# Where the reciprocals of the softmax denominators are taken: on columns before a transpose, or on rows after it

## The chip, the cores and the metric

The kernel runs on one core of a Trainium2 chip. Each core has a matrix engine (TensorE, "PE" in the profile, with its weight loads "PEld"), a vector engine (VectorE, "DVE"), an activation engine (ScalarE, "ACT"), a general engine (GpSimd, "POOL") and a queue that here issues all DMAs (SyncE, "SP"). Each engine works through its own instructions in the order in which they were written; an instruction that has to wait holds up all that stand behind it on its engine. The metric is the device time of one execution in microseconds.

## The reference

A clustered attention is followed by two gated feed-forward layers. The change lies in the attention, of which this is the end (2 batches, 8 heads, 768 tokens, head size 64):

```python
scores = np.where(mask, scores, -1000000000.0)
scores = scores - np.max(scores, axis=-1, keepdims=True)
attn = np.exp(scores)
attn = attn / (np.sum(attn, axis=-1, keepdims=True) + 1e-09)
return np.matmul(attn, v).astype(np.float32)
```

The two layers behind it (1536 tokens of width 512; 2048 and 1536 hidden features) take most of the time and are not touched.

## The kernel before, in words

The attention takes its heads in 8 pairs. A pair is worked in two halves of 384 query rows, so there are 16 halves, and a half in 6 steps: 3 blocks of 128 query rows for each of the two heads. That gives 96 steps, numbered n = 0 to 95 here; two of them make one turn of the loop at L558.

Step n puts on the engines, in this order:
- `scores` (L341): PE forms 128 x 768 scores in PSUM, in one of two buffers `s_ps`; L347 and L351 are its matmuls.
- `maximum` (L356): DVE takes the row maxima from PSUM (L359).
- `transposes` (L395) of step n - 2: PE transposes the exponentials `p` in two groups (L405); ACT copies them out (L410), or DVE copies one group (L408) in some steps.
- `exponentials` (L363): ACT forms exp(s - max), which needs the maximum; its accumulator leaves the row's sum as one column of the tile `st` (L367). The buffer `s_ps` is free after this, so PE's scores of step n + 2 wait for it.

When the 6 steps of a half are through, `st[:, 1, :]` holds 128 x 6 denominators. In step n = 6, 12, ..., 96, `reciprocals` (L372) adds 1e-9 on DVE (L374) and takes the reciprocals of the 128 x 6 tile (L377). One step later (n = 7, 13, ..., 97), `spread` (L379) transposes them on PE to 6 x 128 (L382), copies them on ACT out of PSUM to `rs` (L384), and SP writes them to DRAM (L386). `bring_back` (L389) reads them back, each row over 64 partitions, into `rb`. `normalised` (L422) multiplies a half's output in PSUM by `rb` on DVE (L424), and `split_x` on POOL cuts the result in two parts (L438, L439). A half's output is ready, and L424 stands, at the end of a turn whose second step is n = 13, 19, ..., that is directly behind the `spread` of the following half.

Beside these, `background` (L500) hands out other work by step: loads and splits of the next pair's q and k on POOL (L247 to L266), the cluster masks of the next pair on DVE (L287 to L332), and the first 9 weight blocks of the feed-forward layer (steps in `early`, L496). Such a block is loaded into the only buffer `raw` (L65), shifted by ACT (L69), worked by DVE (L78, L82), and split by POOL (L88, L93). The next block's load waits until L82 is through. The steps n0 of the blocks are 20, 32, 44, 56, 68, 84, 87, 90 and 93: ACT's part stands in step n0, DVE's in n0 + 1 and n0 + 2, after the step's `spread`.

The order of all this is written out by hand; no scheduler changes it.

Of the kernel before, what the change touches and what calls it, by code (L numbers as in the profile page):

```python
# [8 lines left out]
F32 = mybir.dt.float32  # L9
F32R = mybir.dt.float32r  # L10
AF = mybir.ActivationFunctionType
ALU = mybir.AluOpType
# [8 lines left out]
def tile_kernel(ctx, tc, q_t, k_t, q_s, k_s, v_l, cent, w_in, w_out, a_co, b_co, w_gate, w_val, w_o2, out):  # L21
    nc = tc.nc
# [3 lines left out]
    P = 128  # L26
# [12 lines left out]
    def r32(ap):  # L39
        return ap.bitcast(F32)  # L40
# [84 lines left out]
    def pool(stack, name, bufs, side, space=None):  # L125
        kw = {} if space is None else {"space": space}
        return stack.enter_context(tc.tile_pool(name=name, bufs=bufs, side=side, reuse_waits="tile", **kw))

    stage_pools(A, "left", 1, 1)
    base = pool(A, "base", 1, "left")  # L130
# [16 lines left out]
    live = {}  # L147
    pairs = [(b, hp) for b in range(B) for hp in range(H // 2)]
    order = [(b, hp, half, i, e) for b, hp in pairs for half in range(2) for i in range(HB) for e in range(2)]
    PER = 2 * HB  # L150
# [36 lines left out]
    ident = base.tile([P, P], F32, name="ident")  # L187
    make_identity(nc, ident)

    def t_tile(name):  # L190
        return ps_t.tile([P, HB, P], F32, tag="t", name=name)

    def keep_warm(n, to):
        for _ in range(n):
            for j in range(HB):
                nc.tensor.transpose(to[:, j, :], ident, ident)
# [14 lines left out]
    for e in range(2):  # L211
# [2 lines left out]


    sq = base.tile([P, D], F32, name="sq")
    ss = base.tile([P, 4], F32, name="ss")
    nc.vector.memset(ss[:, 3:4], 1e-36)
    nc.scalar.activation(out=sq, in_=cn, func=AF.Square, accum_out=ss[:, 0:1])
    nc.scalar.activation(out=ss[:, 1:2], in_=ss[:, 0:1], func=AF.Ln, bias=ss[:, 3:4])  # L220
# [3 lines left out]
        out=ss[:, 2:3], in0=ss[:, 0:1], scalar=ss[:, 2:3], in1=ss[:, 1:2], op0=ALU.mult, op1=ALU.add  # L224
# [7 lines left out]
    for e in range(2):  # L232
        nc.vector.tensor_copy(
            out=ct[e * D:(e + 1) * D, :, e, :], in_=ct_ps.rearrange("p (h e c) -> p h e c", e=2, c=NC)[:, :, e, :]
# [106 lines left out]
    def scores(b, hp, half, i, e):  # L341
        t = heads[b, 2 * hp + e]
        s_ps = ps_s.tile([P, S], F32, tag="s", name="s_ps")
        q0 = half * HALF + i * P
        qs = slice(q0, q0 + P)
        for lo, hi in CUT:
            nc.tensor.matmul(s_ps[:, lo:hi], t["q1"][:, qs], t["k1"][:, lo:hi], start=True, stop=False)  # L347
        if (b, hp, half, i, e) == order[0]:
            keep_warm(1, fill)
        for lo, hi in CUT:  # L350
            nc.tensor.matmul(s_ps[:, lo:hi], t["q2"][0:KM, qs], t["k2"][0:KM, lo:hi], start=False, stop=True)  # L351
        if (i, e) == (0, 0):
            live["st", b, hp, half] = st_p.tile([P, 3, PER], F32, tag="st", name="st")
        live["s", b, hp, half, i, e] = s_ps

    def maximum(b, hp, half, i, e):  # L356
        st = live["st", b, hp, half]
        k = e * HB + i
        nc.vector.tensor_reduce(  # L359
            out=st[:, 0, k:k + 1], in_=live["s", b, hp, half, i, e], axis=AX.X, op=ALU.max, negate=True  # L360
        )

    def exponentials(b, hp, half, i, e):  # L363
        st = live["st", b, hp, half]
        k = e * HB + i
        p = live["p", b, hp, half, i, e] = p_p.tile([P, S], F32, tag="p", name="p")
        nc.scalar.activation(  # L367
            out=p, in_=live.pop(("s", b, hp, half, i, e)), func=AF.Exp, bias=st[:, 0, k:k + 1],
            accum_out=st[:, 1, k:k + 1],
        )  # L370

    def reciprocals(b, hp, half):  # L372
        st = live["st", b, hp, half]
        nc.vector.tensor_scalar(  # L374
            out=st[:, 1, :], in0=st[:, 1, :], scalar1=1.0, scalar2=1e-9, op0=ALU.mult, op1=ALU.add
        )
        nc.vector.reciprocal(out=st[:, 2, :], in_=st[:, 1, :])  # L377

    def spread(b, hp, half):  # L379
        st = live.pop(("st", b, hp, half))  # L380
        r_ps = t_tile("r_ps")[0:PER, 0, :]
        nc.tensor.transpose(r_ps, st[:, 2, :], ident)  # L382
        rs = rs_p.tile([PER, P], F32, tag="rs", name="rs")
        nc.scalar.copy(out=rs, in_=r_ps)  # L384
        rd = tc.dram_tile([2, HALF], F32, name="rd")
        nc.sync.dma_start(out=rd.rearrange("e (i p) -> (e i) p", p=P), in_=rs)  # L386
        live["rd", b, hp, half] = rd

    def bring_back(b, hp, half):  # L389
        rd = live.pop(("rd", b, hp, half))  # L390
        rb = live["rb", b, hp, half] = rb_p.tile([P, HALF], F32, tag="rb", name="rb")
        for e in range(2):
            nc.sync.dma_start(out=rb[e * D:(e + 1) * D, :], in_=rd[e:e + 1, :].to_broadcast([D, HALF]))

    def transposes(b, hp, half, i, e, on_dve):  # L395
        p = live.pop(("p", b, hp, half, i, e))
        if i == 0:
            live["pt", b, hp, half, e] = pt_p.tile([P, NB, HALF], F32, tag="pt", name="pt")
        pt = live["pt", b, hp, half, e]
        qc = slice(i * P, (i + 1) * P)  # L400
        for g in range(2):
            t_ps = t_tile("t_ps")
            for j in range(HB):
                kb = g * HB + j
                nc.tensor.transpose(t_ps[:, j, :], p[:, kb * P:(kb + 1) * P], ident)  # L405
            ks = slice(g * HB, (g + 1) * HB)
            if g == 1 and on_dve:
                nc.vector.tensor_copy(out=pt[:, ks, qc], in_=t_ps)  # L408
            else:
                nc.scalar.copy(out=pt[:, ks, qc], in_=t_ps)  # L410
# [11 lines left out]
    def normalised(b, hp, half):  # L422
        x = live["x", b, hp, half] = x_p.tile([P, HALF], F32, tag="x", name="x")
        nc.vector.tensor_tensor(  # L424
            out=x, in0=live.pop(("o", b, hp, half)), in1=live.pop(("rb", b, hp, half)), op=ALU.mult
        )

    def split_x(b, hp, half):
        x = live.pop(("x", b, hp, half))
        done = 0  # L430
        while done < HALF:
            t, o = divmod(b * S + half * HALF + done, T)
            n = min(HALF - done, T - o)
            if t not in x_hl:
                x_hl[t] = xy.tile([P, 2, NCC, T], F32R, tag="xy", name="xhl")
            hi = x_hl[t][:, 0, hp, o:o + n]
            src = x[:, done:done + n]
            nc.gpsimd.tensor_scalar(out=hi, in0=src, scalar1=1.0, scalar2=0.0, op0=ALU.mult, op1=ALU.add)  # L438
            nc.gpsimd.tensor_tensor(out=x_hl[t][:, 1, hp, o:o + n], in0=src, in1=r32(hi), op=ALU.subtract)  # L439
            done += n  # L440
# [7 lines left out]
    for e, t in enumerate((h0, h1)):  # L448
# [6 lines left out]
            out=t["k2"][0:D, :], in0=xk1[0:D, :] if e else xk, in1=r32(t["k1"][0:D, :]), op=ALU.subtract  # L455
# [7 lines left out]
        out=h0["q1"][up, :], in0=xs[0][0:D, :], scalar=scale, in1=r32(h0["q1"][0:D, :]),  # L463
        op0=ALU.mult, op1=ALU.subtract,
# [85 lines left out]
    def next_weighted():  # L550
        if pv:
            step = pv.pop(0)
            weighted(*step)
            if step[3] == NB - 1:
                return step[:3]


    for n0 in range(0, len(order) + LAG, 2):  # L558
        for n in (n0, n0 + 1):
            if n < len(order):  # L560
                scores(*order[n])
                maximum(*order[n])
            if n == 1:
                keep_warm(3, fill)
            if n >= LAG:
                transposes(*order[n - LAG], n % (2 * PER) in dve_evac)
            if n < len(order):
                exponentials(*order[n])
            if n % PER == 0 and n:
                reciprocals(*order[n - 1][:3])  # L570
            if n % PER == 1 and n > 1:
                spread(*order[n - 2][:3])
            if n % PER == BB and n > PER:
                bring_back(*order[n - BB - 1][:3])
            for engine in ("dma", "pe", "dve", "pool", "act"):
                background(n, engine)
        finished = next_weighted()
        finished = next_weighted() or finished
        if finished:
            normalised(*finished)  # L580
            split_x(*finished)
        if n >= LAG and (n - LAG) % PER == PER - 1:
            pv.extend([order[n - LAG][:3] + (kb,) for kb in range(NB)])
# [275 lines left out]
```

## Time and profile before

| what | value |
|---|---|
| median of 3 runs | 815.94 us (814.78 to 818.19) |
| the profiled execution | 815.9 us |
| its span, first to last instruction | 814.1 us |
| granted TensorE clock | 1.0 of full speed over the span |
| PE busy | 790.4 us (97%) |
| DVE busy | 592.6 us (73%) |
| ACT busy | 454.0 us (56%) |
| POOL busy | 329.9 us (41%) |

The attention fills about the first 240 us of the span. PE is nearly always busy, so the time is set by PE and by those places where PE stands still for another engine. A row of the timeline gives the start, the duration, the engine, the line, the operation with its tiles, and in brackets the idle time of that engine just before and what ended it.

### The profile page before, as it was taken

The page shows a single profiled execution, that of the slowest core. Times are in us where ns is not written, and L with a number is a line of the kernel's source. Part 1 is how long each engine was busy: PE and PEld are TensorE (multiplying, and loading weights), DVE is VectorE, ACT ScalarE, POOL GpSimd, SP SyncE. Part 2 cuts the span into 40 slices and gives each one's busy share as a digit, 9 for nine tenths or more (in the row PEclk, how much of TensorE's full clock was granted, in tenths as well). Part 3 has the DMA queues.
Part 4 walks back from the last instruction along what each step waited for, and adds up shares of the span by engine and source line. Part 5 has one row for each costly group of instructions (what it writes and reads, how often), then busy time and mean ns, then how long its engine had stood idle before and what let it go on. Part 6 is the DMA issues. An engine that isn't in the chain of part 4 may idle for free.

```text
span 814.1 us, 10999 instructions
## 1 busy us (share of the span) xinstructions
PE 790.4 (97%) x3912; PEld 614.3 (75%) x3912; DVE 592.6 (73%) x888; ACT 454.0 (56%) x862; POOL 329.9 (41%) x286
## 2 busy tenths in 40 slices
PE   5999999999999899999999999999999999999998
PEld 4766666666667788878878787888888888888886
DVE  6888788778559999999999989775545564533435
ACT  5777766777767788777776768544222232221111
POOL 3666585678232333545453343322223332321112
PEclk9999999999999999999999999999999999999999
DMA  5366335533223221220312001311121211100004
GB/s 162 112 204 198 118 113 191 175 107 121 74 96 125 78 75 57 76 75 30 104 52 77 2 27 52 104 53 65 67 77 52 77 53 52 52 27 1 1 2 154
DMA packets 26551, 67.91 MB, mean 83 GB/s; under 512 B 4448, under 2 KB 9536, under 8 KB 26496
## 3 DMA queue, kind: packets, MB, share of 16 engines
q1 hardware_dynamic: 26496, 67.21, 25.0%
q8 instruction: 31, 0.51, 0.3%
q14 instruction: 24, 0.20, 0.1%
HBM read 59.48 MB, written 3.19 MB: 77 GB/s over the span
## 4 chain that ended last, share of the span: by engine, by line
PE 70%; DVE 22%; ACT 3%; issue 3%; POOL 2%; DMA 1%; DVEq 0%; POOLq 0%; ACTq 0%
PE h_ps L617 30%; PE acc L693 19%; PE o_ps L416 7%; PE t_ps L405 5%; PE s_ps L347 4%; PE s_ps L351 3%; DVE td L653 3%; DVE td L656 2%; DVE g L650 2%; DVE tq L636 2%; DVE st L359 2%; DVE tp L639 2%; DVE c L78 2%; DVE h_ps L640 2%; ACT p L367 1%
## 5 line engine op out<-in xcount | busy, mean ns | idle before, releaser
L617 PE MATMUL h_ps<-yhl,w 128*128 128x512 f32 x864 | 202.0, 389 | 0.0
L617 PEld LDWEIGHTS h_ps<-yhl,w 128*128 128x128 f32 x864 | 162.0, 188 | 34.1 <-DVE yhl L725 0.3
L693 PE MATMUL acc<-g,w 128*128 128x512 f32 x576 | 141.7, 392 | 7.3 <-POOL g L661 7.0
L617 PE MATMUL h_ps<-xhl,w 128*128 128x512 f32 x576 | 138.6, 390 | 0.0
L93 POOL TENSOR_TENSOR w<-c,w 128x512 fp32r<-128x512 f32 x68 | 94.1, 1384 | 103.1 <-ACT w L90 102.4
L693 PEld LDWEIGHTS acc<-g,w 128*128 128x128 f32 x576 | 107.1, 188 | 34.2 <-POOL g L661 11.5
L617 PEld LDWEIGHTS h_ps<-xhl,w 128*128 128x128 f32 x576 | 107.9, 188 | 24.1 <-issue 1.8
L359 DVE TENSOR_REDUCE st<-s_ps 128x1 f32<-128x768 f32 x96 | 91.2, 951 | 31.3 <-PE s_ps L351 30.8
L661 POOL TENSOR_TENSOR g<-td,tr 128x512 fp32r<-128x512 f32 x46 | 59.6, 1296 | 130.9 <-DVE td L656 119.9
L693 PE MATMUL acc<-w,g 128*128 128x512 f32 x432 | 103.3, 389 | 0.0
L709 POOL TENSOR_TENSOR part<-ts,part 128x512 f32<-128x512 f32 x34 | 46.0, 1372 | 134.0 <-ACT ts L708 133.8
L708 ACT COPY ts<-acc 128x512 f32<-128x512 f32 x34 | 20.0, 590 | 142.6 <-PE acc L693 142.6
L367 ACT ACTIVATE p<-s_ps,st 128x768 f32<-128x768 f32 x96 | 87.5, 912 | 20.3 <-DVE st L359 19.3
L693 PEld LDWEIGHTS acc<-w,g 128*128 128x128 f32 x432 | 81.1, 188 | 16.8
L410 ACT COPY pt<-t_ps 128x384 f32<-128x384 f32 x160 | 70.1, 484 | 33.9 <-PE t_ps L405 33.6
L711 DVE TENSOR_TENSOR part<-acc,part 128x512 f32<-128x512 f32 x38 | 26.0, 686 | 82.5 <-PE acc L693 82.4
L405 PE MATMUL t_ps<-ident,p 128*128 128x128 f32 x576 | 79.1, 273 | 0.9 <-ACT pt L410 0.8
L416 PE MATMUL o_ps<-pt,v 128*64 128x384 f32 x384 | 72.3, 498 | 0.0
L405 PEld LDWEIGHTS t_ps<-ident,p 128*128 128x128 f32 x576 | 66.8, 141 | 6.2 <-ACT pt L410 1.0
L347 PE MATMUL s_ps<-k,q 128*128 128x512 f32 x192 | 58.8, 387 | 2.0 <-ACT p L367 1.8
L82 DVE SCALAR_TENSOR_TENSOR c<-raw,c 128x512 uint32<-128x512 uint32 x68 | 57.8, 849 | 2.0
L347 PEld LDWEIGHTS s_ps<-k,q 128*128 128x128 f32 x192 | 28.7, 189 | 34.6 <-ACT pt L410 15.6
(105 smaller groups left out, 1051.8 us busy)
## 6 DMA issues: line engine op xcount, KB each, us to landing
raw<-w_in_dram SPq DMA_DIRECT2D x16, 512.0 KB
raw<-w_out_dram SPq DMA_DIRECT2D x16, 512.0 KB
raw<-w_gate_dram SPq DMA_DIRECT2D x12, 512.0 KB
raw<-w_val_dram SPq DMA_DIRECT2D x12, 512.0 KB
raw<-w_o_dram SPq DMA_DIRECT2D x12, 512.0 KB
xq<-q_t_dram SPq DMA_DIRECT2D x14, 384.0 KB
xk<-k_t_dram SPq DMA_DIRECT2D x14, 384.0 KB
sq<-q_s_dram SPq DMA_DIRECT2D x8, 384.0 KB
```

Source lines behind the costliest of these rows:

```text
L82: nc.vector.scalar_tensor_tensor(out=cb, in0=t["low"].bitcast(U32), scalar=29, in1=cb, op0=ALU.logical_shift_right, op1=ALU.bitwise_or)
L93: nc.gpsimd.tensor_tensor(out=w[:, 1, :], in0=t["c"], in1=r32(w[:, 0, :]), op=ALU.subtract)
L347: nc.tensor.matmul(s_ps[:, lo:hi], t["q1"][:, qs], t["k1"][:, lo:hi], start=True, stop=False)
L359: nc.vector.tensor_reduce(out=st[:, 0, k:k + 1], in_=live["s", b, hp, half, i, e], axis=AX.X, op=ALU.max, negate=True)
L367: nc.scalar.activation(out=p, in_=live.pop(("s", b, hp, half, i, e)), func=AF.Exp, bias=st[:, 0, k:k + 1], accum_out=st[:, 1, k:k + 1],)
L405: nc.tensor.transpose(t_ps[:, j, :], p[:, kb * P:(kb + 1) * P], ident)
L410: nc.scalar.copy(out=pt[:, ks, qc], in_=t_ps)
L416: nc.tensor.matmul(live["o", b, hp, half][e * D:(e + 1) * D, :], heads[b, 2 * hp + e]["v"][:, kb, :], live["pt", b, hp, half, e][:, kb, :] ...
L617: nc.tensor.matmul(h_ps, w[:, wi, cs], x[:, xi, cc, :], start=(n == 0), stop=(n == 3 * NCC - 1))
L661: spread.tensor_tensor(out=g[:, 1, :], in0=td, in1=tr, op=ALU.mult)
L693: nc.tensor.matmul(acc[c], lhs, rhs, start=(first and m == 0), stop=(last and m == 2))
L709: nc.gpsimd.tensor_tensor(out=pt[:, c, :], in0=ts, in1=pt[:, c, :], op=ALU.add)
```

## The change

The transpose now takes the denominators themselves. ScalarE adds the constant in the copy out of PSUM (Identity with a bias of 1e-9 from a column filled once), and VectorE takes the reciprocals of the 6 x 128 rows in place. The function `reciprocals` and its call go; lines behind it move up by 3 to 5.

```diff
-    ss = base.tile([P, 4], F32, name="ss")
+    ss = base.tile([P, 5], F32, name="ss")
+    tiny = ss[:, 4:5]
+    nc.vector.memset(tiny, 1e-9)
...
-    def reciprocals(b, hp, half):
-        st = live["st", b, hp, half]
-        nc.vector.tensor_scalar(
-            out=st[:, 1, :], in0=st[:, 1, :], scalar1=1.0, scalar2=1e-9, op0=ALU.mult, op1=ALU.add
-        )
-        nc.vector.reciprocal(out=st[:, 2, :], in_=st[:, 1, :])
...
-        nc.tensor.transpose(r_ps, st[:, 2, :], ident)
+        nc.tensor.transpose(r_ps, st[:, 1, :], ident)
         rs = rs_p.tile([PER, P], F32, tag="rs", name="rs")
-        nc.scalar.copy(out=rs, in_=r_ps)
+        nc.scalar.activation(out=rs, in_=r_ps, func=AF.Identity, bias=tiny[0:PER, :])
+        nc.vector.reciprocal(out=rs, in_=rs)
...
-            if n % PER == 0 and n:
-                reciprocals(*order[n - 1][:3])
```

On VectorE, at the end of the first half (steps 6 to 9), these instructions stood before; `st<-s_ps` is a row maximum, `sm` and `mx` are the mask work of the next pair:

```order
L374 TENSOR_SCALAR st<-st 128x6
L377 RECIPROCAL st<-st 128x6
L315 TENSOR_REDUCE mx<-sm 128x24
L359 TENSOR_REDUCE st<-s_ps 128x1
L318 TENSOR_TENSOR sm<-wt,mx 128x384
L324 TENSOR_SCALAR sm<-sm,msk 128x384
L359 TENSOR_REDUCE st<-s_ps 128x1
L408 COPY pt<-t_ps 128x3x128
```

And these stand there now, from the same reduction of `sm` on:

```order
L317 TENSOR_REDUCE mx<-sm 128x24
L361 TENSOR_REDUCE st<-s_ps 128x1
L381 RECIPROCAL rs<-rs 6x128
L320 TENSOR_TENSOR sm<-wt,mx 128x384
L326 TENSOR_SCALAR sm<-sm,msk 128x384
L361 TENSOR_REDUCE st<-s_ps 128x1
L405 COPY pt<-t_ps 128x3x128
```

Two instructions ahead of a maximum went, and the reciprocal of the rows came in behind that maximum; it waits for ScalarE's copy.

On VectorE, at the end of the fifteenth half (steps 90 to 92), where a weight block (`c<-raw`) is worked too, these stood before:

```order
L374 TENSOR_SCALAR st<-st 128x6
L377 RECIPROCAL st<-st 128x6
L359 TENSOR_REDUCE st<-s_ps 128x1
L78 TENSOR_SCALAR c<-raw 128x512
L424 TENSOR_TENSOR x<-o_ps,rb 128x384
L359 TENSOR_REDUCE st<-s_ps 128x1
L408 COPY pt<-t_ps 128x3x128
L82 SCALAR_TENSOR_TENSOR c<-raw,c 128x512
```

And these stand there now, behind the maximum of step 91:

```order
L381 RECIPROCAL rs<-rs 6x128
L78 TENSOR_SCALAR c<-raw 128x512
L421 TENSOR_TENSOR x<-o_ps,rb 128x384
L361 TENSOR_REDUCE st<-s_ps 128x1
L405 COPY pt<-t_ps 128x3x128
L82 SCALAR_TENSOR_TENSOR c<-raw,c 128x512
```

The reciprocal now stands ahead of both halves of the block's work and of the next maximum. On PE and ACT the instructions stand in the same order as before. SP's write of `rs` stands where it stood and now waits for VectorE instead of ScalarE.

## Rows read from the trace of the kernel before

**Rows 1.** What PE waited for, 20 to 240 us: total, times, longest

```profile
PE r_ps L382 <- DVE st L377: 1.8, 3, 0.8
```

**Rows 2.** DVE groups by form, 0 to 262 us: count, busy us, mean ns, idle before

```profile
L359 DVE TENSOR_REDUCE st<-s_ps 128x1 f32<-128x768 f32 x96 | 91.2, 951 | 31.3 <-PE s_ps L351 30.8
...
L424 DVE TENSOR_TENSOR x<-o_ps,rb 128x384 f32<-128x384 f32 x16 | 8.9, 557 | 12.3 <-issue 6.3 <-PE o_ps L416 3.2 <-POOL q L258 2.0
...
L374 DVE TENSOR_SCALAR st<-st 128x6 f32<-128x6 f32 x16 | 6.6, 410 | 0.1
...
L377 DVE RECIPROCAL st<-st 128x6 f32<-128x6 f32 x16 | 3.1, 191 | 0.6
...
L222 DVE RECIPROCAL ss<-ss 128x1 f32<-128x1 f32 x1 | 0.2, 164 | 1.2 <-ACT ss L221 1.2
```

**Rows 3.** Line L374 alone: durations in ns, least, median and most

```profile
L374 DVE TENSOR_SCALAR st<-st x16: 153/160/1554, 28.4 to 236.8; 128x6 f32<-128x6 f32 x16
```

**Rows 4.** ACT groups by form, whole span

```profile
L635 ACT ACTIVATE tp<-h_ps,coef 128x512 f32<-128x512 f32 x48 | 37.2, 774 | 0.5 <-POOL part L709 0.5
...
L708 ACT COPY ts<-acc 128x512 f32<-128x512 f32 x34 | 20.0, 590 | 142.6 <-PE acc L693 142.6
...
L384 ACT COPY rs<-r_ps 6x128 f32<-6x128 f32 x16 | 3.8, 239 | 0.0
```

**Rows 5.** Timeline at the end of half 5: start, duration, engine, line

```profile
83.57 1.82 POOL L258 TENSOR_TENSOR q<-xq,q 64x768 fp32r<-64x768 f32 x1
...
83.88 1.54 DVE L374 TENSOR_SCALAR st<-st 128x6 f32<-128x6 f32 x1
...
85.78 0.27 PE L382 MATMUL r_ps<-ident,st 128*6 128x128 f32 x1 [0.78 <-DVE st L377]
```

**Rows 6.** Timeline at the end of half 9

```profile
144.56 0.24 ACT L384 COPY rs<-r_ps 6x128 f32<-6x128 f32 x1
...
145.05 0.96 DVE L359 TENSOR_REDUCE st<-s_ps 128x1 f32<-128x768 f32 x1 [0.25 <-PE s_ps L351]
...
148.29 0.92 ACT L367 ACTIVATE p<-s_ps,st 128x768 f32<-128x768 f32 x1
...
149.79 0.61 PE L347 MATMUL s_ps<-k,q 128*128 128x512 f32 x2
```

**Rows 7.** Timeline at the end of half 1

```profile
31.06 0.24 ACT L384 COPY rs<-r_ps 6x128 f32<-6x128 f32 x1
...
32.34 1.81 POOL L266 TENSOR_TENSOR k<-xk,k 64x768 fp32r<-64x768 f32 x1
32.39 0.94 DVE L359 TENSOR_REDUCE st<-s_ps 128x1 f32<-128x768 f32 x1
...
34.46 0.62 PE L347 MATMUL s_ps<-k,q 128*128 128x512 f32 x2 [0.16 <-ACT p L367]
```

**Rows 8.** Timeline at the end of half 14

```profile
213.50 0.24 ACT L384 COPY rs<-r_ps 6x128 f32<-6x128 f32 x1
...
215.18 0.68 DVE L82 SCALAR_TENSOR_TENSOR c<-raw,c 128x512 uint32<-128x512 uint32 x1
...
219.56 0.65 ACT L69 ACTIVATE raw<-raw 128x512 f32<-128x512 f32 x1 [1.75 <-DMA raw<-w_in_dram]
...
220.63 0.55 PE L405 MATMUL t_ps<-ident,p 128*128 128x128 f32 x3 [0.76 <-ACT pt L410]
```

**Rows 9.** Timeline at the end of half 15

```profile
226.86 0.43 DVE L78 TENSOR_SCALAR c<-raw 128x512 uint32<-128x512 uint32 x1 [0.97 <-ACT raw L69]
...
228.04 0.96 DVE L359 TENSOR_REDUCE st<-s_ps 128x1 f32<-128x768 f32 x1 [0.29 <-PE s_ps L351]
...
228.29 0.24 ACT L384 COPY rs<-r_ps 6x128 f32<-6x128 f32 x1
...
229.38 0.68 DVE L82 SCALAR_TENSOR_TENSOR c<-raw,c 128x512 uint32<-128x512 uint32 x1
...
233.59 0.69 ACT L69 ACTIVATE raw<-raw 128x512 f32<-128x512 f32 x1 [1.58 <-DMA raw<-w_in_dram]
```

## The prediction, made before the changed kernel was run

> **What bounds the kernel now.** I read the busy table first: PE works 97% of the span, so a microsecond counts only where PE stands still for it. Next came the list of what PE waits for in the attention. One line touches the change: the transpose of the reciprocals waited for DVE's reciprocal three times, 1.8 us in all [rows 1]. Then I took DVE's groups by shape for prices [rows 2, 3], and last the timeline at each of the 16 places where a half ends, to see what stands behind the new instruction and how long PE can do without it [rows 5 to 9]. The reader is to see there a loop with about a microsecond of room: PE's scores of a step need the buffer that the exponential two steps back gives free, and that needs the row maximum. A maximum that comes up to a microsecond late usually costs nothing; a later one moves PE.
>
> **What goes.** Sixteen L374 and sixteen L377 leave DVE. Their busy time is 6.6 and 3.1 us [rows 2], but L374 takes 0.16 us at the median and 1.55 at most [rows 3]: at half 5 it lasts from 83.88 to 85.42, and POOL's L258 beside it ends at 85.39 [rows 5]. It is held up for as long as that POOL instruction runs. PE waited 0.78 us at that place [rows 5]; the same picture comes back at half 7, and these two make 1.6 of the 1.8 us. So the removal can give 1.8 us, nothing at the other places, where PE's transpose did not wait for DVE. The transpose itself then waits only for ACT's sums, which are long there.
>
> [...]
>
> **What comes: the price of a row reciprocal.** No 6 x 128 reciprocal is in the trace. One element per partition takes 164 ns, six take 191 [rows 2]: 5.4 ns for each further one, so 128 take 191 + 122 x 5.4 = 850 ns. Below, the rate of the row maximum, 951/768 = 1.24 ns an element, gives 0.34 us. Above, the 38 ns by which six reciprocals exceed the shortest L374 (153 ns [rows 3]), spread over six, are 6.3 ns, with 1.24 for the pass 7.6 ns: 1.12 us. I take 0.85, since it alone comes from two rows of the same operation.
>
> [...]
>
> ACT's copy with a bias: the copy of 6 x 128 takes 239 ns, an Identity with scale and bias over 512 columns 774 against 590 for a copy of them [rows 4]. So 0.24 to 0.31 us; I take 0.24. The added memset comes once, at the start, where DVE waits for the first DMA anyway: nothing. The write of `rs` leaves SP a microsecond or two later; its reader L424 comes a half later, and it is hidden unless that grows to several us.
>
> **What moves: DVE now waits for ACT.** The reciprocal stands behind the maximum of step 6m + 1 and waits for ACT's copy, which stands behind that step's exponential. So DVE, which before went on at once with L424 or the mask work, stands idle until the copy is through and then works 0.85 us more. Place by place:
>
> *Halves 14 and 15* (steps 85 and 91) have a weight block behind the reciprocal. At half 15 the copy ends at 228.53, the reciprocal at about 229.43. L78, L424, a maximum, a 384-column copy and L82 follow; before, L78 to L82 took 226.86 to 229.38, of which 0.29 was a wait for PE, so 2.23 [rows 9]. L82 then starts at 231.66 instead of 229.38, 2.28 us late. Its end frees `raw`, the next load starts, and ACT stood 1.58 us for that load at 233.59 [rows 9]; the transposes' copies stand behind it on ACT. So I count 2.25. At half 14 the copy ends at 213.74, the reciprocal at 214.64, L82 starts at 216.87 instead of 215.18 [rows 8]: 1.7 us, and there too ACT stood 1.75 us for the load and PE then 0.76 us for ACT [rows 8]. Both count whole: 1.7 + 2.25 = 3.95.
>
> *Half 1* has the mask work L318 and L324 behind the reciprocal. The copy ends at 31.30, the reciprocal at 32.2. POOL's L266 is due at 32.34 and lasts 1.81 [rows 7]. L318 reads SBUF as L374 does, and I let one of L318 and L324 be held until L266 ends, near 34.1; the rest takes 0.4 more. The next maximum starts near 34.5 instead of 32.39 [rows 7], 2.1 late; PE already waited for this exponential at 34.46 [rows 7]. Cost 2.1. A reciprocal of 0.34 or of 1.12 us meets the same L266: 2.0 to 2.2.
>
> *Odd halves 9 and 11* (with a weight block one step on): the copy ends at 144.80, the reciprocal at 145.70, L424 (0.56 [rows 2]) at 146.2, so the next maximum comes at 146.15 instead of 145.05, 1.1 late [rows 6]. ACT hands this on through the block's shift: the exponential at 148.29 ends at 149.2, PE needs it at 149.79 [rows 6]. So 0.55 of 1.1 shows: 1.1 for both. At halves 5 and 7 the same delay is 0.8, since the maximum before it comes earlier without L374; 0.25 shows: 0.5 for both against their gain of 1.6. Half 3 comes out even, half 13 has no block and room enough.
>
> *Even halves 2 to 12*: the mask work and L424 come about 1.05 late, which the room takes up. But the step L306 behind them competes with POOL's L258 of 1.82 us (the same instruction as in [rows 5]). In four of the six it was held up by it already and ends when it ended. In halves 2 and 8 it had gone ahead; it may now fall behind, for anything from 0 to 1.8 us each. I take 0.3 each, 0.6: mostly it still gets in between.
>
> *Half 16*: DVE waits for PE's output there in any case: nothing.
>
> **Sum.** 3.95 + 2.1 + 1.1 + 0.5 + 0.6 - 1.8 = 6.45 us. The profiled execution took 815.9, the median of the runs 815.94, so nothing is to be shifted: 815.9 + 6.4 = 822.3. With a reciprocal of 0.34, halves 14 and 15 lose 0.5 each, 9 and 11 keep 0.1 between them, 5 and 7 nothing and the competition nothing: 2.95 + 2.0 + 0.1 - 1.8 = 3.25, 819.1. With 1.12 and a copy of 0.31, 0.34 more at each place that shows: 4.65 + 2.2 + 1.8 + 1.2 + 3.6 - 1.8 = 11.65, 827.5.
>
> **The rivals.**
> *All of it is hidden.* Halves 1, 14 and 15 make most of the sum. If at 1 the mask work slips in ahead of L266, and at 14 and 15 PE's room takes up the later load, the removal's 1.8 us are left: 814.1, within 0.5% and not slower. For it speaks that DVE idles 31 us before its maxima [rows 2]; against it that ACT stood for the very load that now starts later [rows 8, 9]. It decides from the point where L82 ends less than about half a microsecond late.
> *L374 and L377 were dearer than PE's waits show.* If all 9.7 us of them [rows 2] had held up maxima and the stop behind ACT fell into idle time, two thirds would come back: about 809.5. Against it: 14 of the 16 L374 lie outside PE's large waits [rows 1].
> [...]
> *The activation doesn't do as the copy did:* were Identity in another table than Exp, ACT would load tables. L635 uses Identity between Abs and Ln in the first layer, so no chance worth a number.
>
> **How the numbers follow.** A difference under 0.5%, 4 us, can't be told from no change: faster is below 811.9, slower above 820.0. Forecast with its own range 819.1 to 827.5: 0.56, of which 0.09 lie under 820.0. The divide of 1.2 us: 0.12. All hidden: 0.25, within. Dearer L374: 0.07, faster. So slower 0.59, same 0.34, faster 0.07. The range goes from 814.0, which takes in the hidden case, to 826.5.
>
> **What would show it.** In the profile after: the reciprocal of the rows at 0.85 us (0.34 to 1.2), always with an idle time on DVE ended by ACT's copy; no wait of PE's r_ps for DVE; the maximum of step 8 near 34.5; L82 of halves 14 and 15 about 1.7 and 2.3 us later against the steps around them, with ACT standing longer for the load. The forecast is wrong if the reciprocal is short, or if the attention's end (PE's first L617, behind half 16) comes less than 3 us later than before.

## The result, and the profile after

The changed kernel took 824.85 us (median of 4 runs, 823.81 to 826.34), the kernel before 815.36 us in the runs beside it (4 runs, 813.27 to 818.19). The ratio is 1.011, with a 95% interval of 1.0086 to 1.0133: slower by 7.0 to 10.8 us. The forecast was 822.3 us, slower, range 814.0 to 826.5. So the direction and the range held; the loss came out at about 9 us instead of the 6.45 worked out.

The profiled execution after took 824.27 us (span 822.4). From its page, the busy times:

```profile
PE 792.8 (96%) x3912; PEld 615.8 (75%) x3912; DVE 591.5 (72%) x873; ACT 454.6 (55%) x862; POOL 331.3 (40%) x286
```

DVE has 1 us less to do than before, and the kernel is slower. No engine has a larger share of the span; PE stands still for 29.6 us of it (822.4 less 792.8), before for 23.7. The next view, what PE waited for between 20 and 250 us (total, times, longest), answers to [rows 1]:

```profile
PE s_ps L349 <- ACT p L369: 5.3, 9, 1.3
PE t_ps L402 <- ACT pt L407: 1.4, 1, 1.4
PE t_ps L402 <- ACT p L369: 0.8, 2, 0.4
PE o_ps L413 <- DVE x L421: 0.3, 1, 0.3
```

Beside the line of [rows 1], the same view of the kernel before (20 to 240 us) had these:

```profile
PE s_ps L347 <- ACT p L367: 1.4, 5, 0.5
PE t_ps L405 <- ACT pt L410: 0.8, 1, 0.8
PE r_ps L382 <- ACT p L367: 0.2, 1, 0.2
```

In all that is 4.2 us before and 7.8 after. The wait of the transpose `r_ps` for DVE is gone, as foreseen. In its place PE's scores wait 5.3 us, where they waited 1.4, for exponentials that give their buffers free late. What made those late stands among DVE's groups by form, which answer to [rows 2]:

```profile
L361 DVE TENSOR_REDUCE st<-s_ps 128x1 f32<-128x768 f32 x96 | 90.8, 948 | 22.7 <-PE s_ps L353 22.2
L381 DVE RECIPROCAL rs<-rs 6x128 f32<-6x128 f32 x16 | 15.1, 941 | 26.4 <-ACT rs L380 23.6 <-DMA xq<-q_t_dram 2.8
L421 DVE TENSOR_TENSOR x<-o_ps,rb 128x384 f32<-128x384 f32 x16 | 8.2, 510 | 0.0
```

The row reciprocal takes 941 ns, and ahead of the sixteen of them DVE stands 26.4 us, nearly all of it ended by ACT's copy. Before, DVE had its idle time ahead of the maxima, waiting for PE (31.3 us), and ahead of L424 (12.3 us); now 22.7 and 0.0. About half of DVE's idle time has moved from places where DVE was ahead of PE to places where DVE is behind ACT. ACT's copy itself has grown (ACT's groups by form; answers to [rows 4]):

```profile
L380 ACT ACTIVATE rs<-r_ps,ss 6x128 f32<-6x128 f32 x16 | 5.5, 344 | 0.0
```

Place by place, from the timeline after. Half 1, which answers to [rows 7]:

```profile
32.27 1.82 POOL L268 TENSOR_TENSOR k<-xk,k 64x768 fp32r<-64x768 f32 x1
...
32.42 0.34 ACT L380 ACTIVATE rs<-r_ps,ss 6x128 f32<-6x128 f32 x1
...
32.79 0.94 DVE L381 RECIPROCAL rs<-rs 6x128 f32<-6x128 f32 x1 [1.42 <-ACT rs L380]
...
34.94 0.95 DVE L361 TENSOR_REDUCE st<-s_ps 128x1 f32<-128x768 f32 x1
...
37.03 0.62 PE L349 MATMUL s_ps<-k,q 128*128 128x512 f32 x2 [1.27 <-ACT p L369]
```

The copy starts 1.36 us later than before (32.42 against 31.06; a lag from the start, for which see the last section), the maximum of step 8 2.55 us later (34.94 against 32.39). Half 1 has cost 1.2 us, and PE waits 1.27 us where it waited 0.16.

By half 9 the copy is 1.41 us late, by half 14 2.13 us (145.97 and 215.63 against 144.56 and 213.50, [rows 6, 8]): the halves between gave back 0.4 us. Then half 14, which answers to [rows 8]:

```profile
215.63 0.34 ACT L380 ACTIVATE rs<-r_ps,ss 6x128 f32<-6x128 f32 x1
...
216.00 0.94 DVE L381 RECIPROCAL rs<-rs 6x128 f32<-6x128 f32 x1 [2.18 <-ACT rs L380]
...
218.94 1.02 DVE L82 SCALAR_TENSOR_TENSOR c<-raw,c 128x512 uint32<-128x512 uint32 x1
...
223.61 0.65 ACT L69 ACTIVATE raw<-raw 128x512 f32<-128x512 f32 x1 [1.69 <-DMA raw<-w_in_dram]
...
224.68 0.55 PE L402 MATMUL t_ps<-ident,p 128*128 128x128 f32 x3 [1.41 <-ACT pt L407]
```

And half 15, which answers to [rows 9], with the first matmul of the feed-forward layer in the last row:

```profile
232.38 0.34 ACT L380 ACTIVATE rs<-r_ps,ss 6x128 f32<-6x128 f32 x1
...
232.75 0.94 DVE L381 RECIPROCAL rs<-rs 6x128 f32<-6x128 f32 x1 [2.82 <-ACT rs L380]
...
235.12 1.44 POOL L436 TENSOR_TENSOR xhl<-x,xhl 128x384 fp32r<-128x384 f32 x1
...
235.69 1.41 DVE L82 SCALAR_TENSOR_TENSOR c<-raw,c 128x512 uint32<-128x512 uint32 x1
...
239.11 0.62 PE L349 MATMUL s_ps<-k,q 128*128 128x512 f32 x2 [1.05 <-ACT p L369]
...
240.60 0.68 ACT L69 ACTIVATE raw<-raw 128x512 f32<-128x512 f32 x1 [1.54 <-DMA raw<-w_in_dram]
...
246.24 0.96 PE L612 MATMUL h_ps<-xhl,w 128*128 128x512 f32 x3
```

The same matmul in the kernel before:

```profile
239.48 0.73 PE L617 MATMUL h_ps<-xhl,w 128*128 128x512 f32 x2
```

L82 ends at 219.96 and 237.10; before, at 215.86 and 230.06 [rows 8, 9]. That is 4.10 and 7.04 us late: 1.97 us came on at half 14 (4.10 less the 2.13 it arrived with), 2.94 at half 15. The attention as a whole ends 6.76 us later (246.24 against 239.48). ACT's halts for the load didn't grow (1.69 and 1.54 us, before 1.75 and 1.58), since the exponentials in front of them on ACT are late as well: on DVE the next maximum stands right behind L82, and those of steps 87 and 93 start 4.11 and 7.05 us later than before. So what L82 loses is passed on twice, by the load and by the maximum. The chain of waits after, around half 15 (start, duration, what), shows how the delay gets there:

```profile
232.50 0.23 ACT rs L380
...
232.75 0.06 DVE rs L381
...
233.97 0.46 DVE x L421
234.43 0.88 DVE st L361
...
235.39 0.99 ACT p L369 x2
236.38 0.76 ACT pt L407 x2
...
237.17 3.34 DMA raw<-w_in_dram
```

ACT's copy, the reciprocal, L421, the maximum, the exponential, and then the load: one line of descent, and PE's scores wait 0.44 and 1.05 us for exponentials on it. That the chain has ACT's L407 ahead of the load rests on some hundredths of a microsecond: `raw` is freed by L82, which ended at 237.10, and the issue follows 0.07 us later.

### The profile page after: what moved, and what is told of

Read it like the earlier page. It is cut to its first block, busy times and chain, and to the rows that moved or that the text cites. A ratio compares the mean times of both kernels' runs of the same rounds, so it can differ in the third digit from the quotient of the medians.

```text
span 822.4 us, 10986 instructions
## 1 busy us (share of the span) xinstructions
PE 792.8 (96%) x3912; PEld 615.8 (75%) x3912; DVE 591.5 (72%) x873; ACT 454.6 (55%) x862; POOL 331.3 (40%) x286
## 4 chain that ended last, share of the span: by engine, by line
PE 63%; DVE 20%; ACT 7%; issue 4%; DMA 3%; POOL 2%; SPq 0%; DVEq 0%; ACTq 0%; POOLq 0%
PE h_ps L612 29%; PE acc L688 19%; PE o_ps L413 4%; PE t_ps L402 4%; ACT p L369 3%; PE s_ps L349 3%; DVE td L648 2%; PE s_ps L353 2%; DVE td L651 2%; DVE g L645 2%; DVE tq L631 2%; ACT pt L407 2%; DVE tp L634 2%; DVE h_ps L635 2%; DVE c L78 2%
## 5 line engine op out<-in xcount | busy, mean ns | idle before, releaser
L361 DVE TENSOR_REDUCE st<-s_ps 128x1 f32<-128x768 f32 x96 | 90.8, 948 | 22.7 <-PE s_ps L353 22.2
L407 ACT COPY pt<-t_ps 128x384 f32<-128x384 f32 x160 | 70.3, 486 | 33.5 <-PE t_ps L402 33.2
L402 PE MATMUL t_ps<-ident,p 128*128 128x128 f32 x576 | 79.8, 274 | 2.2 <-ACT pt L407 1.4
L402 PEld LDWEIGHTS t_ps<-ident,p 128*128 128x128 f32 x576 | 67.4, 142 | 7.6 <-ACT p L369 1.7
L349 PE MATMUL s_ps<-k,q 128*128 128x512 f32 x192 | 59.2, 390 | 5.8 <-ACT p L369 5.3
L82 DVE SCALAR_TENSOR_TENSOR c<-raw,c 128x512 uint32<-128x512 uint32 x68 | 58.9, 866 | 2.0
L349 PEld LDWEIGHTS s_ps<-k,q 128*128 128x128 f32 x192 | 28.9, 190 | 40.8 <-ACT p L369 18.2
```

Of the source, the lines that this page charges most:

```text
L82: nc.vector.scalar_tensor_tensor(out=cb, in0=t["low"].bitcast(U32), scalar=29, in1=cb, op0=ALU.logical_shift_right, op1=ALU.bitwise_or)
L361: nc.vector.tensor_reduce(out=st[:, 0, k:k + 1], in_=live["s", b, hp, half, i, e], axis=AX.X, op=ALU.max, negate=True)
```

## The experiments

The theory: what costs is DVE's stop behind ACT's copy, not the 0.94 us of the reciprocal, and halves 14 and 15 pay most of it. The rivals: the longer reciprocal as such, ACT's dearer copy, or the memset at the start. (That `rs` is written to DRAM later is no cause: L421, which needs it, has no idle time ahead of it.) The first four kernels ran on one chip (kernel before: 816.15 us, 23 runs), the next three on one (816.08 us, 29 runs), the last two on one (815.78 us, 23 runs).

**The wait alone.** The kernel before, with a reciprocal of one element of `rs` behind `spread`: DVE stops as in the changed kernel, and works 0.15 us.

```diff
         nc.scalar.copy(out=rs, in_=r_ps)
+        nc.vector.reciprocal(out=probe, in_=rs[0:1, 0:1])
```

> The kernel before with a reciprocal of one element (0.16 us) of the copied rows added on VectorE where the changed kernel has its row reciprocal: the wait for ScalarE's copy without the 0.94 us. By the theory that wait and work together use up the room, and that halves 14 and 15 count whole, the wait alone costs 0.9 to 1.5 us at halves 14 and 15 and about 1 at half 1: 818 to 820. If the long reciprocal alone matters, 815.5 to 816.5.

Measured: 820.77 us (4 runs), ratio 1.0059 (1.0038 to 1.0081), so 3.1 to 6.6 us, and above the 818 to 820 expected. DVE's group of that line in its profile:

```profile
L386 DVE RECIPROCAL ss<-rs 1x1 f32<-1x1 f32 x16 | 2.4, 151 | 22.3 <-ACT rs L385 22.3
```

The stops are as long as in the changed kernel (22.3 against 23.6 us ended by ACT). Half 1 shows what the prediction said of it, with little of the start's lag (its copy is 0.37 us later than before):

```profile
32.52 2.00 POOL L267 TENSOR_TENSOR k<-xk,k 64x768 fp32r<-64x768 f32 x1
32.87 1.86 DVE L325 TENSOR_SCALAR sm<-sm,msk 128x384 f32<-128x384 f32 x1
34.65 0.94 DVE L360 TENSOR_REDUCE st<-s_ps 128x1 f32<-128x768 f32 x1
```

L325 fell behind POOL's instruction and ended 0.2 us after it; the maximum starts 2.26 us late, 1.9 of it from this half. Halves 14 and 15 together cost 2.6 us in this profile. What follows: the wait without the work makes the kernel slower; and since ACT's copy is the old one here (239 ns), it does so without a dearer copy.

**The work alone.** The kernel before, with a 6 x 128 reciprocal of a constant tile at the same place, which waits for nothing.

```diff
         nc.scalar.copy(out=rs, in_=r_ps)
+        nc.vector.reciprocal(out=ones, in_=ones)
```

> The kernel before with a 6 x 128 reciprocal of a constant tile added at the same place: 0.94 us of work on VectorE, with no wait in front. By the theory that the room of a microsecond takes it up except at halves 1, 14 and 15: 815.5 to 818. If the long reciprocal alone makes the loss: 821 to 824.

Measured: 816.56 us (10 runs), ratio 0.9998 (0.9976 to 1.002). Its 16 reciprocals take 929 ns at the median (900 to 931) and have no idle time ahead of them. What follows: DVE has room for 15 us more; within 2 us either way the work as such is free. The parts don't add up, though. Wait alone makes about 4.8 us, work alone nothing, and the changed kernel 9 us although it also has the gain of the removal. My reading is that behind the stop the room is used up, so that there the work counts, and with it the 0.1 us by which ACT's copy has grown; no run separates these two.

**The same work, one step later.** The changed kernel with the reciprocal of the rows moved behind the next step's other work, when ACT's copy is long through; its write to DRAM goes along.

```diff
-        nc.vector.reciprocal(out=rs, in_=rs)
+        live["rs", b, hp, half] = rs
+    def invert(b, hp, half):
+        rs = live.pop(("rs", b, hp, half))
+        nc.vector.reciprocal(out=rs, in_=rs)
...
+            if n % PER == 2 and n > PER:
+                invert(*order[n - 3][:3])
```

> The changed kernel with one move: the reciprocal of the rows stands one step later on VectorE (behind the work of step 6m + 2), where ScalarE's copy has long ended. The same instructions, the same 0.94 us each, but no wait. If the time is lost to the wait in front of the reciprocal and to what queues behind it (my theory), most of the 9 us come back: 815 to 818. If it is lost to the longer reciprocal itself, 821 to 824. If it comes from the start of the kernel (clock, memset), 823 to 825.

Measured: 818.95 us (10 runs), ratio 1.003 (1.0009 to 1.0051) against the changed kernel's 1.011: some 6 of the 9 us are back, less than expected (815 to 818). Its group, and half 15:

```profile
L385 DVE RECIPROCAL rs<-rs 6x128 f32<-6x128 f32 x16 | 14.9, 930 | 0.0
```

```profile
228.25 0.34 ACT L380 ACTIVATE rs<-r_ps,ss 6x128 f32<-6x128 f32 x1
...
229.11 0.85 DVE L82 SCALAR_TENSOR_TENSOR c<-raw,c 128x512 uint32<-128x512 uint32 x1
229.89 0.93 DVE L385 RECIPROCAL rs<-rs 6x128 f32<-6x128 f32 x1
```

L82 is back at its old place and the reciprocal stands behind it, with no idle time. Same instructions, same durations, other place: no stop, and most of the loss is gone. Not all: the median still lies 0.3% above the kernel before, and L374 is gone here too, which by itself takes the ratio to 0.9973 (below). Against that, some 4.6 us are missing. In its profile the first matmul behind the attention comes 0.4 us earlier than before (239.06), and PE's waits in the attention are 2.7 us, against 7.8 in the changed kernel and 1.7 without L374. Part of what is missing may go with the granted clock (0.993 to 0.998 in its runs, 0.993 to 1.000 in those of before: at 0.998 its two runs took 815.63 and 818.03 us, and the eleven of before 815.44 at the median). No run separates the rest (the dearer copy is still in this kernel); it stays open.

**Only halves 14 and 15 the old way.**

```diff
+    def old_way(b, hp, half):
+        return ((b, hp), half) in ((pairs[-2], 1), (pairs[-1], 0))
...
+        old = old_way(b, hp, half)
+        nc.tensor.transpose(r_ps, st[:, 2 if old else 1, :], ident)
...
+        if old:
+            nc.scalar.copy(out=rs, in_=r_ps)
```

(with `reciprocals` and its call kept for these two).

> The changed kernel with halves 14 and 15 done as before. The maxima of the profile after fall back by 2.0 us at half 14 and 2.9 at half 15; if these are the price of the two weight blocks behind the reciprocal, 4 to 5 us come back: 819.5 to 821. If all halves pay alike, 1.2: 823.5. If the start is the cause: 824 to 825.

Measured: 819.57 us (8 runs), ratio 1.004 (1.0021 to 1.0059) against 1.011: two halves of sixteen pay some 5 to 6 of the 9 us. Its L82 of half 15 starts 0.72 us behind ACT's copy (231.36 and 230.64), in the changed kernel 3.31 us.

**The memset alone.** The changed kernel's profile shows a lower clock at the start (0.64 of full speed from 17 to 25 us, last section), so its one new instruction there was tried by itself in the kernel before.

```diff
-    ss = base.tile([P, 4], F32, name="ss")
+    ss = base.tile([P, 5], F32, name="ss")
+    tiny = ss[:, 4:5]
+    nc.vector.memset(tiny, 1e-9)
```

> The kernel before with the fifth column and its memset alone (0.06 us on VectorE before the first DMA lands). The profile after shows a lower granted clock between 10 and 25 us and its third maximum 1.5 us late, the profile before does not; the separate runs of the kernel before show mean clocks from 0.993 to 1.0 with times from 813 to 820. If the dip at the start varies from run to run whatever the kernel: the same as before, 815 to 817.5, in runs of every clock. If the memset or the column brings it: 817.5 to 819, all runs at 0.993 to 0.996.

Measured: 816.81 us (12 runs), ratio 1.0006 (0.999 to 1.0023): no difference that can be told.

**The reciprocal straight from PSUM.** The changed kernel without ACT's copy; it leaves the 1e-9 out of the computation.

```diff
-        nc.scalar.activation(out=rs, in_=r_ps, func=AF.Identity, bias=tiny[0:PER, :])
-        nc.vector.reciprocal(out=rs, in_=rs)
+        nc.vector.reciprocal(out=rs, in_=r_ps)
```

> The changed kernel with the reciprocal taken straight from the transposed rows in PSUM: ScalarE's copy goes, and with it the addition of 1e-9 is left out. VectorE then waits for PE's transpose alone, which at most halves ends about when the maximum in front does; the work stays at 0.9 us. If the wait for ScalarE is what costs: 814 to 818. If the position and the 0.9 us cost: 820 to 824.

Measured: 813.41 us (12 runs), ratio 0.9969 (0.9951 to 0.9986): faster than before, and just below the 814 to 818 expected. DVE's group and, in a second view, PE's waits from 20 to 240 us:

```profile
L380 DVE RECIPROCAL rs<-r_ps 6x128 f32<-6x128 f32 x16 | 14.9, 933 | 1.2 <-PE r_ps L378 1.2
```

```profile
PE s_ps L349 <- ACT p L369: 0.9, 4, 0.5
PE t_ps L401 <- ACT pt L406: 0.9, 1, 0.9
PE t_ps L401 <- ACT p L369: 0.2, 1, 0.2
```

The reciprocal is as long as in the changed kernel and at the same place in the order. It waits for PE's transpose instead of ACT's copy, 1.2 us instead of 26.4, and PE's waits in the attention fall from 7.8 to 2.0 us. This is the plainest evidence for the wait. It also takes 16 copies, 5.5 us, off ACT; but the last kernel below gives ACT 4.8 us of other work in their place and is as fast, so it is not ACT's work that cost.

**What the removal gives.** Two kernels from the kernel before: one lets ACT add the 1e-9 to the 128 x 6 columns behind the sixth exponential (Identity, 299 ns) in place of DVE; the other drops the addition (it leaves the 1e-9 out).

```diff
+    def add_tiny(b, hp, half):
+        st = live["st", b, hp, half]
+        nc.scalar.activation(out=st[:, 1, :], in_=st[:, 1, :], func=AF.Identity, bias=tiny)
...
-        nc.vector.tensor_scalar(
-            out=st[:, 1, :], in0=st[:, 1, :], scalar1=1.0, scalar2=1e-9, op0=ALU.mult, op1=ALU.add
-        )
...
+            if n % PER == PER - 1 and n < len(order):
+                add_tiny(*order[n][:3])
```

> The kernel before, with the addition of 1e-9 on the 128 x 6 columns moved from VectorE (L374) to ScalarE, right behind the sixth exponential; the reciprocal stays on columns. It takes away the hold of L374 behind POOL, worth up to 1.8 us by PE's waits, and adds 0.2 us of ScalarE 16 times at places where it has room. By my theory 813.5 to 816, that is 0 to 2 us under the kernel before. If ScalarE's work is on the path: 817 to 819.

> The kernel before without VectorE's addition of 1e-9 on the columns (that addition is left out of the computation), nothing else changed. If the gain of the kernels that run faster than before comes from the removal of that one instruction, which was held behind GpSimd up to 1.55 us, this one alone takes 1.5 to 3 us off: 813.5 to 815, ratio 0.996 to 0.9985. Rival, the gain comes from the row form (short transposes' path, reciprocal later): within 0.5 us of the kernel before.

Measured: 814.58 us (12 runs), ratio 0.9981 (0.9963 to 0.9999), and 814.0 us (12 runs), ratio 0.9973 (0.9956 to 0.999). The one instruction L374 is worth 2.2 us (0.8 to 3.6); as ACT's work it costs nothing that can be told.

**Both together, complete.** ACT adds the 1e-9 to the columns as above, PE transposes the denominators, DVE takes the reciprocal of the rows from PSUM. Against the first of those two kernels (its `reciprocals` and the call go too):

```diff
-        nc.tensor.transpose(r_ps, st[:, 2, :], ident)
+        nc.tensor.transpose(r_ps, st[:, 1, :], ident)
...
-        nc.scalar.copy(out=rs, in_=r_ps)
+        nc.vector.reciprocal(out=rs, in_=r_ps)
```

> The complete computation: ScalarE adds the 1e-9 to the 128 x 6 columns, TensorE transposes these denominators, VectorE takes the reciprocal of the rows straight from PSUM; the instruction on the columns and ScalarE's copy of the rows both go. By the theory of the wait (the loss is VectorE's stop behind ScalarE's copy, the 0.94 us of the reciprocal are free) it comes out with the two kernels that have this in part, which took 813.4 and 814.6 us: 812.5 to 814.8, ratio 0.996 to 0.999. Rival, the work on VectorE counts after all where nothing else is saved: at or above the kernel before, 816 to 818 us. In the profile the row reciprocal should have no idle time ended by ScalarE.

Measured: 813.82 us (12 runs), ratio 0.9971 (0.9957 to 0.9986). It computes all of the reference, beats the kernel before by 2.4 us and, by the ratios (0.9971 and 1.011), the changed one by about 11. It is no faster than dropping L374 alone (ratio 0.9973): the row form adds nothing to the gain, and without the stop it takes nothing from it.

## Why the prediction was right, and where it fell short

**The mechanism** was the one forecast: DVE stands behind ACT's copy, and what is queued behind the reciprocal comes late. Of its signs, the idle time ahead of the reciprocals, the vanished wait of `r_ps` for DVE, the late L82 and the attention's end over 3 us late (6.76) are there. One is not: ACT doesn't stand longer for the load. The prediction followed the late L82 to the load alone; the maximum that stands behind L82 is late too, and takes ACT and PE along. That the whole delay counts came true all the same. The wait-only kernel and the one that reads PSUM show it without the other parts.

**The price of the row reciprocal**: 0.85 us forecast, 0.94 measured. With the row of six elements (191 ns), 941 ns for 128 make 6.1 ns for each further element, not 5.4. ACT's copy with a bias took 0.34 us, above the 0.24 to 0.31 allowed for it. The two add 0.2 us at a place.

**Halves 14 and 15** are the largest term, and it was sized too small: 1.7 + 2.25 = 3.95 forecast, 1.97 + 2.94 = 4.91 in the profile; the kernel with these two undone agrees. L82's start was right: measured from ACT's copy it came 1.63 and 2.22 us later than before. Its end was not, since L82 itself grew from 0.68 to 1.02 and 1.41 us. POOL's L436 cuts the output that L421 has just made, so it moved along with L421, and DVE, which no longer waits for PE between the two, reaches L82 1.79 us after L421's start instead of 2.18; at half 15 it runs from 235.12 to 236.56 and L82, from 235.69, ends 0.54 us behind it. That POOL's instruction is what held L82 is read from this overlap; no run was made on it. The prediction used that very effect for half 1 and for L374, but moved L421 without moving what POOL does with its result.

**Half 1**: 2.1 forecast, with a hold of L318 or L324 estimated from that of L374 [rows 5]; 1.9 with the wait alone. In the changed kernel's profile 1.2, because the half came 1.3 us late and POOL's L268 did not (32.27, before 32.34): a lag that was there already was absorbed by the hold (L320 took 0.84 us and ended at 34.50, 0.41 us behind L268). The maximum came at 34.94, forecast 34.5.

**Halves 2 to 13**: 1.1 + 0.5 + 0.6 less 1.8 = 0.4 forecast, -0.4 in the profile. That looks close, and is partly luck: both sides were too small. The maxima of step 8 and of step 85 bound this stretch. Step 85 before and after, then steps 8 and 85 in the kernel that only drops L374 (second of the two under "What the removal gives"):

```profile
210.73 0.96 DVE L359 TENSOR_REDUCE st<-s_ps 128x1 f32<-128x768 f32 x1
```

```profile
212.87 0.96 DVE L361 TENSOR_REDUCE st<-s_ps 128x1 f32<-128x768 f32 x1 [0.42 <-PE s_ps L353]
```

```profile
32.38 0.94 DVE L359 TENSOR_REDUCE st<-s_ps 128x1 f32<-128x768 f32 x1
...
207.30 0.96 DVE L359 TENSOR_REDUCE st<-s_ps 128x1 f32<-128x768 f32 x1 [0.32 <-PE s_ps L351]
```

The stretch took 178.34 us before, 177.93 in the changed kernel and 174.92 without L374. So by these profiles the removal gave about 3.4 us there instead of 1.8, and the stops cost about 3.0 instead of 2.2. One profile each is rough: in the kernels with the memset alone and with the work alone the stretch differs from before by -0.5 and +0.9. Over whole runs the removal is worth 2.2 us (0.8 to 3.6).

**What the sum did not have.** The profiled pair differs by 8.3 us of span. Start and half 1 together make 2.55 of it (2.1 forecast), halves 2 to 13 -0.4 (0.4), halves 14 and 15 4.9 (3.95), half 16 -0.3 (0), and what lies behind the attention 1.55 (0). The last has two parts: a wait of PE in the first layer, 0.9 us for DVE's `g` against 0.2 before, and the end of the span behind the last matmuls, 0.9 us longer. No experiment was made on either. The kernel with the memset alone, whose attention ends 0.3 us earlier than before, loses 1.5 us behind it too, there with a granted clock of 0.93 from 264 to 288 us; so such an amount comes without the change, and it is not claimed for it. The medians are 9.5 us apart, about 1 us more than the profiled pair; no run separates that.

**The rivals.** "All of it is hidden" fell: PE had no room for the later load and the later maxima at halves 14 and 15. "L374 and L377 were dearer" fell as it was priced (two thirds of 9.7 us); the removal by itself gives 2.2, near the 1.8 of the sum. No run shows a reciprocal of 1.2 us, to which the forecast gives a chance of 0.12 and which it names as the upper end of its sign (0.34 to 1.2): the reciprocal of 6 x 128 took 941 ns in the changed kernel, 930 one step later, 933 straight from PSUM, and 929 at the median with the work alone. ACT loaded no table for the Identity of L380: its ACT_TABLE_LOADs, 1.28 us each, are five before (L42, L646, L647 and twice L678) and the same five after (L42, L641, L642 and twice L673). And the range that held is 12.5 us wide, because it takes in the hidden case as well.

## What to carry to other kernels

An instruction that is cheap in itself but waits for another engine in the middle of an in-order queue costs the room of everything behind it (here sixteen reciprocals of 0.15 us, with 22.3 us of DVE's idle time ahead of them, cost 3.1 to 6.6 us); look whether the same operand can be read one hop earlier (here from PSUM, straight behind the transpose), or put the instruction where its operand is old. When a row of instructions is moved in a forecast, move with it what other engines do with its results, above all what runs beside the instruction one looks at (here POOL's L436 beside L82, which took 1.41 us instead of 0.68 and ended 0.54 us behind it). And a small gain may lie in the instruction that was held (2.2 us for sixteen operations of 0.16 us at the median), not in the larger rearrangement around it.

## What the runs showed of the hardware

*The time of a reciprocal grew with the elements per partition, not with the partitions*: 151 ns for 1 x 1, 164 for 128 x 1, 191 for 128 x 6, 941 for 6 x 128, and 933 for the same straight from PSUM; the row maximum of 128 x 768 takes 948.

*L374 was held to the end of a POOL instruction* at four of its sixteen places, to within 0.03 us of that end (up to 1.55 us in the kernel before, 1.65 in the one with the work alone). *Reciprocals that ran inside a POOL instruction were not held*: L377 took 191 or 192 ns at all sixteen places, five of them inside one, and L381 of half 1, inside POOL's L268 (32.27 to 34.09), 0.94 us as everywhere. L82 (1.02 and 1.41 us instead of 0.68) and the mask step L325 of the kernel with the wait alone (1.86), which also started inside a POOL instruction, ended 0.2 to 0.55 us behind it.

*The granted clock dips in some profiled executions and not in others, in the same two stretches.* Rows of the windows 17 to 25 us and 264 to 288 us (length, PE busy, clock, DMA share, GB/s) of the kernel before, the changed one and the best one:

```profile
17.00:25.00 8.00, 7.32 (x51) 1.00 0.97 335
264.00:288.00 24.00, 21.69 (x95) 1.00 0.23 75
```

```profile
17.00:25.00 8.00, 8.00 (x42) 0.64 0.79 260
264.00:288.00 24.00, 20.99 (x92) 1.00 0.26 88
```

```profile
17.00:25.00 8.00, 7.59 (x45) 0.79 0.92 296
264.00:288.00 24.00, 21.88 (x90) 0.93 0.27 87
```

In the first dip of the changed kernel two matmuls of 128 x 512 take 0.99 us (L349 at 18.86; before, L347 at 19.10, 0.62) and six transposes 1.48 (L402 at 20.29; before, L405 at 19.91, 0.82); from 22.97 us on two such matmuls take 0.62 us there too. Ahead of the first, from 10 to 17 us, PE was busy for 3.61 of 7 us in the changed kernel, for 4.59 in the kernel before and for 4.85 in the best one; in the second it stands 2.1 us for POOL, in all three. The changed kernel's 1.36 us of lag at half 1 go with the first dip. The memset is not needed for it: from 17 to 25 us the clock was 0.79 in the kernel with the wait alone and 0.80 in the one that drops L374, neither of which has the memset, and 1.00 in the one that reads PSUM, which has it. Over whole runs the kernel before has mean clocks of 0.993 to 1.000, with 819.9 us at 0.993 (one run) and 814.7 to 815.2 at 1.000 (three) on the first chip. One profile of each kernel, read end to end, would have put the lag on the change.
